# One transformer block on one Trainium2 core: eight products on zeros ahead of the first loads, K/V products of two tiles split by weight chunk, w_phi loaded from another queue, and a new unit order

## The chip, the cores and the metric

The kernel is one program on one NeuronCore of a Trainium2 chip. Five engines work side by side, each through its own queue of instructions: PE (TensorE, matrix products), DVE (VectorE), ACT (ScalarE), POOL (GpSimd) and SP (SyncE, which here only issues DMA transfers). They wait for one another on semaphores. The metric is the device time of one execution in microseconds; lower is better. Four runs of the kernel before the change gave 288.08, 289.53, 287.90 and 289.26 us, so the median is 288.67 us.

## The reference: what is computed

The input x has 2048 rows (tokens) of 640 values in bf16. Two halves follow one another, each with a layer norm without learned scale and a residual sum.

```
x1  = x + attention(layernorm(x))        # linear attention, 32 heads of 20
out = x1 + glu(layernorm(x1))            # (g * u) @ w_down, no activation

q, k, v = layernorm(x) @ wqkv            # 640 -> 3 * 640
pk      = k_head @ w_phi[head]           # 20 x 20 per head; the same for q
phi     = [softmax(pk), softmax(-pk)]    # 40 features per head
kv      = sum over tokens of phi_k^T v   # 40 x 20 per head, z = sum of phi_k
o       = (phi_q @ kv) / (phi_q @ z + 1e-6), then @ wo
```

The sum over tokens stands between the two parts of the attention: no token's output can be computed before all 2048 tokens have gone through K and V.

## The kernel before, in words

**Tiles.** The 2048 tokens are 16 tiles of 128 rows. The 640 columns of the model are 5 chunks of 128 for contraction; an output of 640 columns is two halves of 320, each in its own PSUM bank (there are 8 banks). The feed-forward part works in five blocks of tokens: 256, 512, 512, 512, 256.

**Units.** `build_graph` describes the work as named units (`G.op`), each with an engine, an emit function, an occupancy, and its reads and writes. The names matter for what follows; a number is a tile unless said otherwise.

- `wk0`, `wk2`, `wk4` load the K columns of wqkv (chunks 0-1, 2-3, 4; 160 KB per chunk), `wv0`, `wv3` the V columns, `x0`, `x1`, `x2`, ... the tokens, all on SP's queue (L259). `phr` and `ph5` load w_phi (L280), from ACT's queue.
- `WT0`..`WT4` (L345) transpose a chunk of the K weights on PE in six pieces; `WTe0`.. copies the result out of PSUM (L228). `F1_0`..`F1_4` (L366) multiply a chunk by the block-diagonal w_phi matrix `Phi`, which POOL builds (`phi0`, `phi5`, L320 and L326); `Fe1_0`.. copies it into the weight tile `Wp`. So the feature map is folded into the K weights once. `F0_0`.. does the same for the Q weights.
- `L1s`, `L1a` (L382, L385, DVE), `L1l`, `L1e` (ACT) and `xn` (L410, DVE) are the layer norm of a tile. Tiles 0 to 2 are transposed on PE (`xt`, L418, copied out by `xte`), the others by a DMA transpose on SP's queue (L426), which writes `xnT`.
- `V` and `K` (L437) are the products of a tile with the V weights and the folded K weights, ten products of 320 columns each. `Ve` copies V out, `Kx` (L455, ACT) takes the two exponentials, `Ks` (L458) and `Kr` (L461, both DVE) sum and invert per head, `Kn` (L463, POOL) scales, and `KV` (L472, PE) adds the tile's contribution to the sum over tokens, which stays in three PSUM banks from tile 0 to tile 15.
- `Q` (L493), `N` (L526), `o`, `O` (L569) and `h` are the second half of the attention; `U` (L608), `g`, `u`, `D` (L626), `y` (L638) and `w` (L640) the feed-forward part. Tile 15's `D` and `y` are made in two halves of 320 columns, so that the last output is small.

**What sets the order.** The order on each engine is not written by hand. `schedule` is a list scheduler: it steps through time, and each engine that is free takes the ready unit with the lowest key; `take` gives it PSUM banks. The keys come from the string `TUNED`, which holds `name:key` or `name:key:1`; the `:1` picks the second engine where a unit has a choice (ACT or DVE for a copy out of PSUM). `schedule` also keeps a counter `bw` for the transfers: the bytes of all DMAs pass one after another at a fixed rate. `emit` then works out the semaphore waits, and each engine runs its list strictly in order. A different table therefore changes every queue, also where no line of code has changed.

**The start before the change.** SP issues x1, x0, x6, wk0, wk2, wv0, x2, wk4, wv3, x4. PE begins with WT1 and WT0, which need wk0. DVE takes the tiles' norms in the order 1, 0, 6, 7, 2, 3, ...

**The loads inside the K/V part.** SP's queue also carries the transposes of tiles 3 to 15 and, between them, the remaining tokens, six transposes of the Q weights (`wqt`), and the weights of the output projection and of gate and up (`wo`, `wg`, `wu`, 320 to 480 KB each), paced by `PACE` so that a load follows a certain transpose.

## Time and profile before

| | before |
|---|---|
| median of four runs | 288.67 us (287.90 to 289.53) |
| the profiled execution's own time | 288.08 us |
| its span | 286.4 us |
| PE busy | 273.3 us, 95% of the span |
| DVE busy | 179.6 us, 63% |
| ACT busy | 105.6 us, 37% |
| POOL busy | 61.4 us, 21% |
| first product on PE | 7.29 us |
| last product's result taken up by DVE | 283.72 us |

The profiled execution took 1.7 us more than its span, which covers what lies around the first and the last instruction. The page gives busy times per engine, the span in 40 slices, and groups of instructions by source line. The chain of waits goes back from the last instruction to whatever released each step. The timeline lists instructions by start and duration, with the idle time before them and what ended it. PE's busy time counts instructions in flight, so neighbours overlap: a single 320-column product is shown with 299 ns, but ten of them in a row take 1.36 us in the chain.

### The profile page before, as it was taken

To read this page: it belongs to the slowest core of one execution; us is meant where nothing else is said; L and a number is where in the kernel's file an instruction comes from. 1 tells how busy PE (TensorE), PEld (TensorE's weight loads), DVE (VectorE), ACT (ScalarE), POOL (GpSimd) and SP (SyncE) were. 2 spreads that over 40 slices of the span, in tenths; PEclk is the share of its full clock that TensorE was granted. 3 is DMA by queue.
4 is the path that set the end of the run, shared out by engine and by line. 5 is a ranking of instruction groups with operands and counts; after the bars stand their busy time and mean duration, and the time that the engine had idled before them with its cause. 6 is when DMAs were issued, how large, how long until landed. Compare 5 with 4: busy or idle time off the path is not lost.

```text
span 286.4 us, 4973 instructions
## 1 busy us (share of the span) xinstructions
PE 273.3 (95%) x2047; PEld 182.2 (64%) x2063; DVE 179.6 (63%) x365; ACT 105.6 (37%) x186; POOL 61.4 (21%) x67
## 2 busy tenths in 40 slices
PE   0999999889999999999999999999999999999996
PEld 0976778668555678855565576544677545667774
DVE  3799799976367978993769825315736725233432
ACT  2877656353777761523204103033101222421010
POOL 7005479689013223000210010000002010000000
PEclk9999999999999999999999999999999999999999
DMA  7548178990002376512133211200022120100101
GB/s 208 208 99 201 51 133 184 269 353 7 0 0 48 62 211 166 79 35 48 25 70 48 46 46 49 69 0 2 1 69 71 46 48 0 24 2 3 66 14 57
DMA packets 44766, 22.31 MB, mean 78 GB/s; under 512 B 35783, under 2 KB 43463, under 8 KB 44743
## 3 DMA queue, kind: packets, MB, share of 16 engines
q1 hardware_dynamic: 43984, 21.96, 31.4%
q8 instruction: 16, 0.26, 0.4%
q10 hardware_dynamic: 759, 0.03, 0.2%
q14 instruction: 7, 0.06, 0.1%
HBM read 11.01 MB, written 2.62 MB: 48 GB/s over the span
## 4 chain that ended last, share of the span: by engine, by line
PE 88%; DMA 5%; DVE 4%; ACT 1%; issue 1%; SPq 0%; DVEq 0%
PE ps L608 36%; PE ps L626 18%; PE ps L437 10%; PE ps L569 8%; PE ps L493 7%; PE ps L526 4%; PE ps L472 3%; DMA xnT<-xn 3%; DMA scratch<-in_A_wqkv_dram 2%; DVE SR L458 2%; PE ps L366 1%; PE ps L345 1%; DVE xn L410 1%; ACT ev L455 0%; SPq L259 0%
## 5 line engine op out<-in xcount | busy, mean ns | idle before, releaser
L608 PE MATMUL ps<-xnT,Wgu 128*128 128x512 bf16 (+1 forms) x588 | 106.2, 335 | 0.6
L608 PEld LDWEIGHTS ps<-xnT,Wgu 128*128 128x128 bf16 x600 | 58.3, 98 | 42.4 <-DVE ev L616 0.8
L613 ACT ACTIVATE scratch<-ps 128x512 bf16<-128x512 f32 (+1 forms) x60 | 30.6, 511 | 95.9 <-PE ps L608 83.8
L616 DVE TENSOR_TENSOR ev<-ps,scratch 128x512 bf16<-128x512 f32 (+1 forms) x60 | 33.4, 575 | 34.7 <-PE ps L608 18.6
L626 PE MATMUL ps<-Wp,ev 128*128 128x320 bf16 x384 | 53.5, 299 | 0.0
L437 PE MATMUL ps<-Wp,xnT 128*128 128x320 bf16 x320 | 46.3, 299 | 2.2 <-DMA xnT<-xn 2.0
L626 PEld LDWEIGHTS ps<-Wp,ev 128*128 128x128 bf16 x384 | 37.5, 98 | 14.7
L463 POOL TENSOR_TENSOR ev<-ev,SR 128x1280 bf16<-128x1280 bf16 x16 | 37.4, 2365 | 27.1 <-DVE SR L461 27.1
L437 PEld LDWEIGHTS ps<-Wp,xnT 128*128 128x128 bf16 x320 | 30.3, 98 | 14.8 <-DMA xnT<-xn 3.6
L638 DVE SCALAR_TENSOR_TENSOR Wp<-ps,rs,x_all 128x640 bf16<-128x640 f32 (+1 forms) x17 | 14.4, 845 | 32.0 <-PE ps L626 32.0
L558 POOL TENSOR_TENSOR scratch<-scratch,sm 128x640 bf16<-128x640 f32 x12 | 15.2, 1270 | 59.3 <-DVE sm L555 41.0
L588 ACT ACTIVATE xn<-x_all,mv 128x640 bf16<-128x640 bf16 x16 | 13.2, 825 | 34.8 <-DVE mv L582 34.8
L458 DVE TENSOR_REDUCE SR<-ev 128x64 f32<-128x1280 bf16 x16 | 23.5, 1469 | 3.7 <-ACT ev L455 3.4
L502 ACT ACTIVATE eqT<-ps 128x512 bf16<-128x512 f32 x40 | 21.6, 594 | 11.2 <-PE ps L493 11.1
L455 ACT ACTIVATE ev<-ps 128x640 bf16<-128x640 f32 x32 | 20.7, 705 | 12.2 <-PE ps L437 11.4
L569 PE MATMUL ps<-Wo,scratch 128*128 128x320 bf16 x160 | 24.0, 299 | 0.0
L583 POOL TENSOR_SCALAR ln<-mv 128x1 f32<-128x1 f32 x16 | 3.3, 208 | 93.8 <-DVE mv L582 92.1
L493 PE MATMUL ps<-xnT,Wp 128*128 128x512 bf16 x96 | 22.8, 379 | 0.2
L569 PEld LDWEIGHTS ps<-Wo,scratch 128*128 128x128 bf16 x160 | 15.5, 98 | 7.0 <-DMA scratch<-scratch 0.3
L526 PEld LDWEIGHTS ps<-KVm,eqT 128*128 128x128 bf16 x192 | 12.9, 98 | 4.4 <-issue 0.2
L573 DVE TENSOR_TENSOR x_all<-ps,x_all 128x640 bf16<-128x640 f32 x16 | 13.1, 820 | 4.1 <-PE ps L569 4.0
L526 PE MATMUL ps<-KVm,eqT 128*128 128x154 bf16 (+1 forms) x192 | 15.5, 221 | 0.1
(51 smaller groups left out, 193.0 us busy)
## 6 DMA issues: line engine op xcount, KB each, us to landing
out_dram<-Wp SPq DMA_DIRECT2D x15, 160.0 KB, 1.8
x_all<-in_A_x_dram SPq DMA_DIRECT2D x7, 320.0 KB, 3.6
Wgu<-in_B_w_gate_dram SPq DMA_DIRECT2D x5, 384.0 KB, 5.7
Wgu<-in_B_w_up_dram SPq DMA_DIRECT2D x5, 384.0 KB, 5.7
Wp<-in_B_w_down_dram SPq DMA_DIRECT2D x4, 480.0 KB, 5.5
scratch<-in_A_wqkv_dram SPq DMA_DIRECT2D x2, 320.0 KB, 5.3
Wp<-in_A_wqkv_dram SPq DMA_DIRECT2D x1, 480.0 KB, 6.6
Wo<-in_A_wo_dram SPq DMA_DIRECT2D x1, 480.0 KB, 4.8
```

Source lines behind the costliest of these rows:

```text
L437: ins = e.matmul(pb(b, hb)[:, 0:320], lhsT=T["xnT"][:, c, P * t:P * (t + 1)], rhs=T["Wp"][:, kind, c, 320 * hb:320 * (hb + 1)], start=(c = ...
L455: G.op("act", "Kx%d_%d" % (t, s), lambda e, s=s, b=b, ek=ek: e.activation(out=T["ek"][:, ek.slots[0], s, :].rearrange("p (b n) -> p b n", ...
L458: G.op("dve", "Ks%d" % t, lambda e, ek=ek, sr=sr: e.tensor_reduce(out=T["SR"][:, sr.slots[0], 0, :], in_=T["ek"][:, ek.slots[0], :, :].rea ...
L463: G.op("pool", "Kn%d" % t, lambda e, ek=ek, sr=sr: e.tensor_tensor(out=T["ek"][:, ek.slots[0], :, :].rearrange("p s (h f) -> p (s h) f", f ...
L493: ins = e.matmul(pb(b)[:, 0:n], lhsT=T["Wp"][:, 0, i, P * c:P * (c + 1)], rhs=T["xnT"][:, i, o0:o0 + n], start=(i == 0), stop=(i == NC - 1))
L502: G.op("act", "Qx%d_%d_%d" % (q, c, s), lambda e, s=s, c=c, o0=o0, n=n, b=b: e.activation(out=T["eqT"][:, s, c, o0:o0 + n], in_=pb(b)[:, 0 ...
L526: ins = e.matmul(pb(b, y)[:, 22 * h0:22 * (h0 + j1 - j0)], lhsT=T["eqT"][:, s, c, P * t:P * (t + 1)], rhs=T["KVm"][:, OFF[s, c] + j0:OFF[s ...
L569: ins = e.matmul(pb(b, hb)[:, 0:320], lhsT=T["oT"][:, oT.slots[0], c, :], rhs=T["Wo"][:, c, 320 * hb:320 * (hb + 1)], start=(c == 0), stop ...
L608: ins = e.matmul(pb(b)[:, 0:n], lhsT=T["Wgu"][:, gu, c, P * ft:P * (ft + 1)], rhs=T["xnT"][:, c, o0:o0 + n], start=(c == 0), stop=(c == NC ...
L613: G.op("act", "g%d_%d" % (bi, ft), lambda e, pg=pg, gt=gt, n=n: e.activation(out=T["gt"][:, gt.slots[0], 0:n], in_=pb(pg)[:, 0:n], func=AF ...
L616: o_ = G.op("dve", "u%d_%d" % (bi, ft), lambda e, pu=pu, gt=gt, hh=hh, ft=ft, n=n: e.tensor_tensor(out=T["hh"][:, hh.slots[0], ft, 0:n], i ...
L626: ins = e.matmul(pb(b, hb)[:, 0:320], lhsT=T["hh"][:, hh.slots[0], ft, P * tt:P * (tt + 1)], rhs=T["Wd"][:, ft, c0 + 320 * hb:c0 + 320 * ( ...
```

## The change

Five things change in the code; the table `TUNED` is replaced as a whole.

1. Before anything else DVE clears a tile `zero` (128x512), and PE makes eight products of 512 columns from it into a PSUM bank that nobody reads (`warm`).
2. The V and K products of tiles 0 and 1 become five units each, one per weight chunk (`V0_0` to `V0_4`, and so on). Each waits for its own chunk of the weights alone. The V weights come in three transfers (2, 2 and 1 chunks) in place of two.
3. `phr` and `ph5` go to SP's queue. `ph5` loads 40 rows in place of 128, into a tile that POOL clears first (`ph50`).
4. Tile 15's last product is cut 320, 192, 128 columns in place of 320, 320.
5. In `schedule` the counter `bw` starts at 2.2 and goes at 240 up to 5.0 and at 370 from there, in place of 340 throughout. The new keys in `TUNED` come from a search with noise.

```diff
+TSPLIT = (0, 1)
+NWARM = 8
+LASTCUT = [(0, 320), (320, 512), (512, 640)]
...
-    for n_, (a, b_) in enumerate(((0, 3), (3, 5))):
+    for n_, (a, b_) in enumerate(((0, 2), (2, 4), (4, 5))):
         dma("sp", "wv%d" % a, lambda a=a, b_=b_: T["Wp"][:, 2, a:b_, :],
...
-    dma("act", "phr", lambda: T["phr"][0:120, :, :],
+    dma("sp", "phr", lambda: T["phr"][0:120, :, :],
...
-    dma("act", "ph5", lambda: T["ph5"][:, :], lambda: T["A_wphi"].rearrange("h d f -> (h d) f")[512:640, :], 5, [ph5_b], key=-99)
+    G.op("pool", "ph50", lambda e: e.memset(T["ph5"][:, :], 0.0), 0.2, LP, [], [ph5_b], -99.2)
+    dma("sp", "ph5", lambda: T["ph5"][88:128, :], lambda: T["A_wphi"].rearrange("h d f -> (h d) f")[600:640, :], 2, [ph5_b],
+        reads=[ph5_b], key=-98.4)
...
+    G.op("dve", "zero", lambda e: e.memset(T["zero"][:, :], 0.0), 0.2, LD, [], [z_b], -200)
+    def warm(e):
+        for _ in range(NWARM):
+            ins = e.matmul(pb(wm_b)[:, 0:512], lhsT=T["zero"][:, 0:P], rhs=T["zero"][:, :], start=True, stop=True)
+        return ins
...
     def proj(kind, t, name, key):
         b = Buf(name, "psum", 2)
+        parts = [(c, c + 1) for c in range(NC)] if t in TSPLIT else [(0, NC)]
+        for c0, c1 in parts:
...
-        G.op("pe", name, f, mm_c(*[320] * 10), LT, [xT_b[t]] + wp_b[kind], [b], key)
+            G.op("pe", name if len(parts) == 1 else "%s_%d" % (name, c0), f, mm_c(*[320] * (2 * (c1 - c0))), LT,
+                 [xT_b[t]] + wp_b[kind][c0:c1], [b], key)
...
-            halves = [(0, 320), (320, 640)] if t == last else [(0, 640)]
+            halves = LASTCUT if t == last else [(0, 640)]
...
-                bw = max(bw, now + 1.5) + o.dma / 340.0
+                bw = max(bw, now + 1.5)
+                bw += o.dma / (240.0 if bw < 5.0 else 370.0)
```

The new orders, as far as they are spoken of below:

- SP: x0, wv4, phr, wk4, x1, ph5, wk2, wk0, wv0, x2, wv2, x4, x6, then the transposes and paced loads; among them xt12, xt13, wg2, wu1, xt14, wu2, wg1, wu3, wg3, xt15.
- PE: warm, WT4, xt0, WT3, F1_4, WT2, WT1, WT0, F1_3, xt1, V0_0, F1_0, V0_1, F1_1, V0_2, F1_2, V0_3, K0_0, V0_4, K1_0, K0_1, K1_1, K0_2, V1_0, K0_3, V1_1, K0_4, V1_2, xt2, V1_3, K1_2, V1_4, K1_3, K2, V2, K3, V3, K1_4, V5, ...; later ... K15, V14, KV12, F0_2, KV13, V15, Q0_4, Q0_1, KV14, Q0_3, KV15, Q0_2, Q0_0, ...
- DVE from Ks0 to Kr10: Ks0, xn5, xn6, xn4, xn7, L1s8, Kr0, ..., Ks5, xn8, Kr5, Ks3, xn11, Kr3, ..., xn9, ..., xn10, ..., Kr7, xn12, xn13, Ks9, Kr8, xn14, Ks10, xn15, Kr10.
- POOL's scalings: Kn0, 2, 1, 5, 3, 4, 6, 7, 8, 10, 9, 11, 12, 13, 14, 15.
- Copies out of PSUM: of the V tiles DVE has tile 15 alone (before: 0, 1, 11, 15); of the Q folds it has none (before: three); of the K folds it has three (before: one).

## The prediction

> **What bounds the kernel now.** I read the busy rows and the 40 slices first, to see which engine fills the span.
>
> ```profile
> span 286.4 us, 4973 instructions
> PE 273.3 (95%) x2047; PEld 182.2 (64%) x2063; DVE 179.6 (63%) x365; ACT 105.6 (37%) x186; POOL 61.4 (21%) x67
> PE   0999999889999999999999999999999999999996
> ```
>
> PE is busy from the second slice to the last, so time can be won only where PE is empty, slow or waiting. The chain of waits shows where.
>
> ```profile
> 2.17 5.06 DMA scratch<-in_A_wqkv_dram
> 7.24 0.05 issue
> 7.29 1.46 PE ps L345 x12
> ...
> 12.14 0.34 PE ps L345 x6
> 12.48 0.29 PE ps L366 x7
> ...
> 18.81 0.60 ACT ev L455
> 19.41 0.02 issue
> 19.44 1.49 DVE SR L458
> ...
> 29.11 0.68 PE ps L472 x12
> 29.80 1.36 PE ps L437 x10
> ...
> 54.99 4.92 DMA xnT<-xn
> 59.90 0.05 issue
> 59.95 1.53 PE ps L437 x10
> ```
>
> PE starts at 7.29, when wk0 lands. Twelve transposes take 1.46 there (0.122 each), six take 0.34 (0.057) at 12.14: PE runs at half rate at first. At 54.99 the chain leaves PE: a tile's transpose ends a wait.
>
> The chain also gives a price for every unit: K or V tile 1.36 (two of its ten products 0.27), KV 0.68, fold 0.29, six weight transposes 0.34, a tile's five transposes 0.28, Q or a 512-token U 1.08, a 256-token U 0.545, N 0.36, O 1.36, D 3.26. I call a unit's start minus the sum of all units before it its **delay**. PE's timeline has K1 at 17.50, after 8.07 of work (5 x 0.34, 3 x 0.28, 5 x 0.29, 3 x 1.36): delay 9.4. Q0_0 starts at 73.51 after 60.9 (32 K and V 43.5, 16 KV 10.9, ten folds 2.9, transposes 2.5, one Q 1.1): delay 12.6. At the end, 283.65, all work is 270.8: delay 12.8. So 9.4 us go at the start, 3.2 in the K/V part, 0.2 in the 210 us after it.
>
> The DVE timeline of the K/V part shows what makes tiles late there.
>
> ```profile
> 48.17 1.10 DVE L410 TENSOR_SCALAR xn<-x_all,mv,rs 128x640 bf16<-128x640 bf16 x1
> 49.19 1.48 DVE L458 TENSOR_REDUCE SR<-ev 128x64 f32<-128x1280 bf16 x1
> 50.58 1.08 DVE L410 TENSOR_SCALAR xn<-x_all,mv,rs 128x640 bf16<-128x640 bf16 x1
> 51.59 1.47 DVE L458 TENSOR_REDUCE SR<-ev 128x64 f32<-128x1280 bf16 x1
> 52.98 0.43 DVE L410 TENSOR_SCALAR xn<-x_all,mv,rs 128x640 bf16<-128x640 bf16 x1
> ```
>
> POOL's timeline shows what ran beside them.
>
> ```profile
> 37.47 14.01 POOL L463 TENSOR_TENSOR ev<-ev,SR 128x1280 bf16<-128x1280 bf16 x6 [5.56 <-DVE SR L461]
> ```
>
> Two normalisations took 1.10 and 1.08 while POOL scaled (until 51.48); the one at 52.98, with POOL idle, took 0.43.
>
> **The start.** Warm products: a clear and eight products of 512 columns; at half rate (0.427 each, four times a cold 128-column one) 3.4 us, all before the first weights. They end near 4.7 and cover nothing else. The half rate cost PE about 2 us: its first 29 transposes and 21 fold products took 4.57 (7.29 to 11.86) against 2.5 at the later prices. What remains of that gain is set by who is late next: the loads.
>
> The loads run one after another. wk0 landed at 7.23 with 960 KB ahead of or in it; wv3, issued at 5.00 with 6.9 to landing, at 11.9, 1600 KB later: 343 KB per us. In the new order wk0 has 1306 KB, 346 more, so it lands at 8.2. The favourable end is issue alone: seven SP issues at about 0.48 from 0.79 put wk0's at 4.15; with a free 160 KB load's 2.3 to landing and 0.45 more for its size, 6.9. I take 8.2, the loaded row; x1, wk4 and wk2 come earlier, so by then PE has done WT4, xt0, WT3, F1_4, WT2.
>
> From wk0 on ACT is late next: two transposes 0.7, copies WTe0, WTe1, xte1, Fe1_0, Fe1_1, Fe1_2 at 0.6 to 0.7 each 3.9, waits 0.4. So K0_2 can start 5.0 after wk0, at 13.2, with 6.1 of work ahead of it: delay 7.1. V0_2 (wv2, 640 KB later, 10.1, with 4.0 ahead) and xt2 (x6, 1600 KB later, 12.9, then 0.8 of statistics and 0.4 of normalising; 7.8 ahead) are covered. K2 also needs xte2, which stands behind Kx0_0 on ACT: 0.3 more. I put the delay at K2 at **7.4** against 9.4, a gain of 2.0 (3.4 with the favourable landing). Moving phr behind wv4 on SP costs its issue, 0.65 by ACT's timeline, inside the 0.48-spaced issues; phi0 waits for it (2.6 to landing from 1.7: 4.3) and stands behind POOL's masks, ready near 6.2, before F1_4. ph5 follows x1 and lands near 5.7; phi5 is now behind phi0. The extra clears (0.2 each) stand before the first x tile on DVE and inside POOL's start.
>
> **The K/V part.** DVE hands over all V copies but one and three Q folds and takes two more K folds: 3 + 3 - 2 = 4 copies of 0.75, 3.0 off DVE and onto ACT, which had over 6 us free of 15 between 30 and 45. But POOL's scalings now collide with more normalisations. Ks0 follows Kx0_0, xte2 and Kx0_1 as before (19.44, 2.0 after K0's end at 17.40); K0_4 has 7.5 ahead, so it ends at 15.0 and Ks0 starts at 17.0. From there to Kr10 DVE has 11 sums at 1.40, 10 reciprocals at 0.46, 12 normalisations at 0.36, 8 tiles' statistics at 0.79 + 0.12 (spacings in the timeline): 31.6. Eight of the normalisations (tiles 8 to 15) now stand where POOL has scalings queued; at the 0.66 that the two rows above lost, 5.3. Bounds: nothing, and 15.3, if each loses a whole scaling (2.35 less its own 0.44). Kr10 then ends at 53.9. POOL does 10, 9, 11, 12, 13 one after another, 5 x 2.33, so KV13 cannot start before 65.7, with 56.4 ahead of it on PE: delay **9.3** against 12.6.
>
> The Trainium skill, "SBUF — State Buffer", section "Who interferes with whom", says that DVE's fast modes and GpSimd share a port pair as an exclusive lock: the later one stands still until the other is done. The rows agree (1.10 from 48.17 ends 0.2 after a scaling's end). By it a normalisation met at random would lose half a scaling, 1.18, eight 9.4, and KV13 would stand at 69.8, delay 13.4, the K/V gain gone and more: a rule that speaks against this change.
>
> Transposes behind weights: xt14 follows wg2 and wu1, xt15 wu2, wg1, wu3, wg3. Before, the transposed tile of the chain landed 4.92 after issue behind three such loads. xn15 ends by 53.2; behind 1536 KB at 343 it lands by 60, and K15 has 52.7 ahead: it asks for a delay of 7.3 only. Hidden.
>
> **After the K/V part** the units are the same and the loss was 0.2; KV15 leaves three Qs before the first N, 3.2 us, where DVE needs 2.1 for the three KVe. I leave 0.2.
>
> **The tail.** The last y took 0.55 for 320 columns, a 640 one 0.89: 128 columns cost 0.35, a gain of 0.2. Cutting 320 in 192 and 128 costs PE 12 x 2.5 ns = 0.03. Nothing hides this; it stands at the end.
>
> Sum: delay 12.8 to 9.5, 3.3, and 0.2 at the tail: 3.5. On the profiled execution 288.08 - 3.5 = 284.6; that one is 0.6 below the median of 288.67, so **285.2** in the terms of the median.
>
> **Rivals.**
> - *No wait in the K/V part*: normalisations fall into POOL's gaps. For it: four of the earlier ones did (34 to 36.8). Delay 7.4 + 0.2 and the favourable landing up to 1.4 less: 12.8 - 7.6 + 0.2 = 5.4, 283.3, down to 281.9.
> - *The zeros do not lift the rate.* PE is nearly empty between 4.7 and 8; if it is at half rate again from wk0 on, up to 2 us of the old loss come back, through Kx0 and Ks0 to all that follows: 287.2. The trace shows one rise only, about 4 us after PE's first work. The Trainium skill, "TensorE: Matmul & The Clock Gate", Part 1, has it that a busy window of about 3.4 us, not counted from the first product, lifts the clock, and an idle one drops it; the rise in the trace agrees, no run here shows the drop. By it the eight products are just one window long, and the sum could be either 285.2 or 287.2.
> - *Slower: DVE stands behind POOL.* Place: normalisations 8 to 15; price: what each loses, times eight, straight to KV13. At 1.2 each the result is before's time; at 1.5 (12 us) Kr10 ends at 60.6, KV13 stands at 72.4, delay 16.0, and the time is 288.67 + 3.4 - 0.2 = 291.9. It decides from 1.35 each. For it: six scalings ran back to back from 37.47. Against: DVE that is held up feeds POOL later, which opens gaps; two of sixteen lost 0.66.
>
> **How the numbers follow.** Half a per cent, 1.4 us, is about what a measurement of this kernel tells from no change: below 287.2 faster, above 290.1 slower. Chances: forecast 0.52 (its own range 284.0 to 286.6); no wait 0.16; half rate 0.12, mostly on the faster side; DVE behind POOL 0.20, of which 0.04 end faster, 0.09 same, 0.07 slower. Faster 0.52 + 0.16 + 0.09 + 0.04 = 0.81, same 0.03 + 0.09 = 0.12, slower 0.07. The range takes in the first two, the half rate and part of the last: 282.4 to 288.4.
>
> **What the profile after would show.** Right: transposes at 0.06 each from the first, WT1 near 8.2, K2 near 16.6, KV13 near 66 ended by POOL's L463, the first N near 76, a last y of 0.35. Wrong: WT1 near 7 or below, 0.107 a transpose after the zeros, normalisations of over 1.5, a wait of PE after 80 us, or PE waiting for a transposed tile for over 1 us.

## The result, and the profile after

The changed kernel takes 289.42 us in the median (286.92 to 291.14, 45 runs), the kernel before 288.97 (286.66 to 291.04, 71 runs, those beside the experiments included). The ratio is 1.0018, with a 95% interval of 1.0003 to 1.0033: if anything slower by 0.2%, where 1.2% of gain was forecast. The forecast was 285.2, so 4.2 us of gain are missing. The profiled execution took 288.29 us against 288.08.

The first lines of the page of the kernel after: span, busy time, and PE's share in 40 slices.

```profile
span 286.6 us, 5018 instructions
PE 276.2 (96%) x2067; PEld 182.1 (64%) x2083; DVE 183.8 (64%) x364; ACT 108.7 (38%) x191; POOL 58.8 (21%) x66
...
PE   6899998999999999999999999997999999999996
```

PE now starts in the first slice (the products on zeros), but there is a new dent in the 28th slice, near 195 us, where PE never waited before.

The chain of waits of the kernel after (start, duration, what it was).

```profile
3.59 4.70 DMA scratch<-in_A_wqkv_dram
...
30.92 2.48 DVE xn L426
...
40.23 3.62 DMA xnT<-xn
43.85 0.05 issue
43.90 1.53 PE ps L455 x10
...
56.24 11.62 POOL ev L484 x5
...
194.17 5.10 DMA scratch<-scratch
199.31 1.53 PE ps L590 x10
```

Four places hold the end up: the load wk2 (landing at 8.29), a normalisation of 2.48 and a transposed tile near 31 to 44, the five scalings of POOL in a row to 67.86, and a transpose of the attention's second half (oT13) that took 5.10.

PE's waits in the same execution (in all, times, longest), those on transposed tiles, on POOL and on oT13:

```profile
PE ps L590 <- DMA scratch<-scratch: 1.7, 1, 1.7
PE ps L455 <- DMA xnT<-xn: 1.4, 2, 0.8
...
PE ps L493 <- POOL ev L484: 0.5, 2, 0.3
```

PE's timeline of the kernel after shows the start (start, duration, count; in brackets the idle time before and what ended it).

```profile
5.09 0.82 PE L361 MATMUL ps<-ident,scratch 128*128 128x128 bf16 x6 [0.26 <-DMA scratch<-in_A_wqkv_dram]
...
8.33 0.51 PE L361 MATMUL ps<-ident,scratch 128*128 128x128 bf16 x6 [1.89 <-DMA scratch<-in_A_wqkv_dram]
...
8.98 1.17 PE L361 MATMUL ps<-ident,scratch 128*128 128x128 bf16 x18
```

WT4 ran at half rate; then PE waited 1.9 for wk2. In this execution the transposes after the wait ran at full rate, eighteen in a little over 1 us.

Where the two profiled executions differ is seen from the delay. Below it is counted product by product, at 0.0558 us for 128 columns, 0.1358 for 320 and 0.2158 for 512, the prices behind the chain's 0.34, 1.36 and 1.08. On this scale the three values that the prediction read for the kernel before (9.4, 12.6, 12.8) are 9.49, 13.05 and 13.66.

| delay at | before | after | forecast change | measured change |
|---|---|---|---|---|
| K2 | 9.49 | 8.30 | -2.0 | -1.2 |
| Q0_0, behind the K/V part | 13.05 | 11.94 | -3.3 | -1.1 |
| O13, near 200 us | 13.61 | 14.13 | -3.3 | +0.5 |
| D14_0, near 279 us | 13.66 | 14.19 | -3.3 | +0.5 |

The tail gives back a little: from the last output's start on DVE to the end of the span it was 2.7 us and is 2.3. So of the 3.8 that are missing at D14_0, 0.8 are lost at the start, 1.4 in the K/V part (it lost 3.6 in both kernels, where 1.9 was forecast) and 1.6 behind it, where the single unit O13, 120 us later, lost 1.8.

### The profile page after: what moved, and what is told of

Its sections match the earlier page's. It is cut to its first block, busy times and chain, and to the rows that moved or that the text cites. A ratio compares the mean times of both kernels' runs of the same rounds, so it can differ in the third digit from the quotient of the medians.

```text
span 286.6 us, 5018 instructions
## 1 busy us (share of the span) xinstructions
PE 276.2 (96%) x2067; PEld 182.1 (64%) x2083; DVE 183.8 (64%) x364; ACT 108.7 (38%) x191; POOL 58.8 (21%) x66
## 4 chain that ended last, share of the span: by engine, by line
PE 81%; DVE 6%; POOL 5%; DMA 5%; ACT 1%; issue 1%; SPq 0%; DVEq 0%; POOLq 0%
PE ps L629 35%; PE ps L648 18%; PE ps L514 7%; PE ps L455 7%; PE ps L590 7%; POOL ev L484 4%; PE ps L547 4%; DVE xn L426 3%; DVE SR L479 2%; DMA scratch<-scratch 2%; DMA scratch<-in_A_wqkv_dram 2%; DMA xnT<-xn 1%; PE ps L493 1%; DVE SR L482 1%; PE ps L382 1%
## 5 line engine op out<-in xcount | busy, mean ns | idle before, releaser
L648 PE MATMUL ps<-Wp,ev 128*128 128x320 bf16 (+2 forms) x396 | 54.0, 295 | 0.0
L484 POOL TENSOR_TENSOR ev<-ev,SR 128x1280 bf16<-128x1280 bf16 x16 | 37.5, 2367 | 28.3 <-DVE mv L401 17.0
L579 POOL TENSOR_TENSOR scratch<-scratch,sm 128x640 bf16<-128x640 f32 x10 | 12.7, 1271 | 123.7 <-DVE sm L576 110.2
L660 DVE SCALAR_TENSOR_TENSOR Wp<-ps,rs,x_all 128x640 bf16<-128x640 f32 (+3 forms) x18 | 14.6, 810 | 26.2 <-PE ps L648 26.1
L560 DVE RECIPROCAL sm<-ps 128x32 f32<-128x32 f32 x16 | 5.6, 352 | 16.0 <-PE ps L547 15.9
L514 PEld LDWEIGHTS ps<-xnT,Wp 128*128 128x128 bf16 x100 | 9.5, 98 | 9.4
L547 PEld LDWEIGHTS ps<-KVm,eqT 128*128 128x128 bf16 x192 | 12.8, 98 | 4.1
```

The source lines that it names most:

```text
L484: G.op("pool", "Kn%d" % t, lambda e, ek=ek, sr=sr: e.tensor_tensor(out=T["ek"][:, ek.slots[0], :, :].rearrange("p s (h f) -> p (s h) f", f ...
L514: ins = e.matmul(pb(b)[:, 0:n], lhsT=T["Wp"][:, 0, i, P * c:P * (c + 1)], rhs=T["xnT"][:, i, o0:o0 + n], start=(i == 0), stop=(i == NC - 1))
L547: ins = e.matmul(pb(b, y)[:, 22 * h0:22 * (h0 + j1 - j0)], lhsT=T["eqT"][:, s, c, P * t:P * (t + 1)], rhs=T["KVm"][:, OFF[s, c] + j0:OFF[s ...
L648: ins = e.matmul(pb(b, hb)[:, 0:w], lhsT=T["hh"][:, hh.slots[0], ft, P * tt:P * (tt + 1)], rhs=T["Wd"][:, ft, c0 + w * hb:c0 + w * (hb + 1 ...
```

## The experiments

### What the zeros do

**Zeros alone.** The kernel before with the clear and the eight products on zeros in front, all else in its order.

```diff
+    G.op("dve", "zero", lambda e: e.memset(T["zero"][:, :], 0.0), 0.2, LD, [], [z_b], -200)
+    G.op("pe", "warm", warm, 0.43 * NWARM, LT, [z_b], [wm_b], -200)
```

> The kernel before with the clear and the eight products on zeros alone; every other unit keeps its place. Theory A (the prediction's): the zeros lift PE's rate before wk0 lands, so the 29 transposes and 21 fold products that took 4.57 us (7.29 to 11.86) take about 2.5 to 3; K1 starts near 15.9 instead of 17.5 unless ACT's copies hold it, and the time falls by 1 to 2 us. Theory B (PE is covered by ACT's copies and by DVE in the K/V part): the first transposes take 0.06 each, but K0 or the K/V part gives the time back, and the time moves by less than 0.5 us. Theory C (the rate does not rise): transposes at 0.12 each as before, no change.

Over its twelve executions the median is 291.85 (286.88 to 296.19), against 289.51 for the kernel before beside them; over the four shortest alone the ratio is 0.9986 (0.9947 to 1.0025). So the zeros alone show no gain. The profiled execution is among the long ones, so the trace is used for its first 13 us alone. PE's timeline there:

```profile
1.24 3.59 PE L347 MATMUL ps<-zero 128*128 128x512 bf16 x8 [1.24 <-DVE zero L342]
6.89 1.46 PE L357 MATMUL ps<-ident,scratch 128*128 128x128 bf16 x12 [2.06 <-DMA scratch<-in_A_wqkv_dram]
```

Twelve transposes still take 1.46, as without zeros. PE stood idle for 2.06 between the zeros and the data. Whether the rate had risen in between, no product shows; when the data came it was half. K1's delay was 9.53 (9.49 before).

**The change without the zeros.**

```diff
-    G.op("pe", "warm", warm, 0.43 * NWARM, LT, [z_b], [wm_b], -200)
```

> The changed kernel without the eight products on zeros; the order of all else is the same. In the changed kernel WT3 started at 8.34 when wk2 landed, at 0.06 a transpose. Theory A: without the zeros PE is at half rate until some 4 us after WT4 (5.1), so until 9 to 12: K2 starts 0.5 to 2 us later than 17.40, and the time rises by as much. Theory B: the load of wk2 and wk0 and ACT's copies set K0_2 whatever the rate; K2 moves by less than 0.5 us and the time stays.

289.84 (288.43 to 292.84), ratio 1.0006 (0.9984 to 1.0029). The delay at K2 is 10.63. So on the changed kernel the zeros can't be told from nothing by the time, although one trace has 2.3 less delay with them. The reason is in the next two runs, which have the changed kernel's start and something else changed later.

**O13 later, and a strided normalisation.** In the first, the order of PE and DVE is held, and only O13 moves behind U2_11_1 and U2_10_1. In the second, the normalisation of tiles 8 to 15 reads and writes every second element, then the others.

```diff
+    # PE, around 195 us: U2_5_1 U2_11_1 U2_10_1 O13 U2_9_1 ... in place of U2_5_1 O13 U2_11_1 U2_10_1 U2_9_1 ...
```

> The changed kernel with O13 two units (2.16 us) later on PE; g2_11 and u2_7 trade places with hc13 and h13. In the changed kernel PE waited 1.7 us before O13 for the transpose of tile 13, which took 5.1 us to land; beside it one instruction packet of 16 KB held a DMA engine for 1.68 us. Theory A: this wait is in every execution, because the packet comes at the same place of the program; with O13 behind two more units it is gone, and the time falls by 1.2 to 1.7 us. Theory B: it was one execution's accident, or the next wait takes its place: less than 0.5 us.

```diff
-            return e.tensor_scalar(out=T["xn"][:, xb.slots[0], :], in0=T["x"][:, t, :],
+            v = (lambda a: a.rearrange("p (n two) -> p two n", two=2)) if t >= 8 else (lambda a: a)
+            return e.tensor_scalar(out=v(T["xn"][:, xb.slots[0], :]), in0=v(T["x"][:, t, :]),
```

> The changed kernel with the normalisations of tiles 8 to 15 reading and writing every second column, first the even, then the odd ones; same values. In the changed kernel four of these eight took 2.48, 1.35, 2.48 and 1.08 us beside POOL's scalings, against 0.44 alone. Theory A (DVE's fast form stands still while POOL scales): in the slow form each takes about 0.75 and none over 1; DVE gains some 3 us before Kr10, KV13 comes 1.5 to 3 us earlier than 67.9, the time falls by as much, less what PE then lacks. Theory B (the long ones are due to something else): they stay long, Kr10 comes later by up to 2 us, and the time rises.

O13 later: 289.04, ratio 0.9985 (0.9959 to 1.0011). Strided: 290.56, ratio 1.0031 (1.0009 to 1.0054). What each shows of its own subject follows below; here it is their start. The busy time by stretches gives PE's granted clock (the column after POOL's). The kernel after:

```profile
8.00:11.00 3.00, 2.67 (x45) 2.35 (x45) 2.12 (x4) 1.49 (x3) 0.00 (x0) 1.00 1.05 364
11.00:14.00 3.00, 3.00 (x36) 1.86 (x36) 3.00 (x10) 3.00 (x7) 0.00 (x0) 1.00 0.41 142
```

The strided kernel in the same stretches:

```profile
8.00:11.00 3.00, 2.76 (x31) 2.77 (x32) 1.65 (x3) 0.81 (x1) 0.00 (x0) 0.59 0.96 330
11.00:14.00 3.00, 3.00 (x44) 2.49 (x42) 2.15 (x5) 2.69 (x5) 0.00 (x0) 0.84 0.42 152
```

0.41 of 3 us and 0.16 of 3 us of the strided kernel's clock are missing: 1.7 us, a stretch of 3.4 us at half rate, right after PE's wait for wk2. Its K2 has a delay of 9.40, that of the run with O13 later 9.37 (its clock is 0.74 and 0.69 in these stretches). That is before's 9.49. Among the 46 listed executions of the changed kernel, 27 have a mean clock of 0.994, which is such a stretch (0.6% of 287 us is 1.7; the mean does not say where it lies), and they take 289.65 in the mean; the 17 with a clock of 1.000 take 288.54. The profiled execution of the changed kernel is one of the lucky ones. The mean is blind to one case, a half rate that lasts from the first product on: three of the executions below have a mean of 1.000 and transposes of 0.107. Seven executions with the changed kernel's loads and eight zeros were profiled in all, two of them with other first units; their delays at K2 are 8.30, 9.08, 9.34, 9.37, 9.40, 10.27 and 10.60, 9.5 in the mean. Only the first kept its rate: in three the clock fell after the wait (9.34, 9.37, 9.40), in three the rate had not risen when wk2 came. Over these seven executions, then, the start gained nothing. A wait of some 2 us went either way: PE's idle time before wk2 was 1.89 in the one that kept its rate, and 1.74, 2.00 and 2.17 in the three that lost it.

The Trainium skill, "TensorE: Matmul & The Clock Gate", Part 1, has the activity window run free of the kernel's start, so that one kernel meets it in different phases. That one order kept its rate, lost it or never had it in these executions agrees; no run here shows the window itself.

**Sixteen zeros,** so that PE is busy until the data come: on the changed kernel and on the kernel before, the orders unchanged.

```diff
-NWARM = 8
+NWARM = 16
```

> The changed kernel with 16 instead of 8 products on zeros, all else in the same order. Theory A, the clock falls back while PE waits: the eight products end at 4.83 and PE then has 1 us of work until wk2 lands at 8.3; in the profiled executions of the strided and the O13 experiments the transposes after that took 0.107 each and K2 stood 1.1 later than in the profiled execution of the changed kernel. Sixteen products keep PE busy until 6.6 to 8.3, so the rate stays up: transposes at 0.056 in the profile, delay at K2 at most 8.4, mean granted clock 1.000 in all timed runs, and a median 0.6 to 1.1 us below that of the changed kernel (ratio to before about 0.999). Theory B, the loads alone set the start: no change, ratio 1.002; or, if the eight more products hold WT4 and xt0 up, up to 1 us more (1.005).

> The kernel before with a clear and 16 products on zeros in front and nothing else changed. With eight of them PE stood idle from 4.9 to 6.9, the first 29 transposes and 21 fold products still ran at half rate and K1 had a delay of 9.53 against 9.49 without. Theory A: sixteen products end near 7 to 8, the rate is up when wk0's transposes start, so they take 0.057, K1's delay falls by 1 to 2 to between 7.5 and 8.5 and the time by as much of it as the K/V part leaves, between 0 (all eaten by later waits there, DVE and POOL being no earlier) and 2.0: 287 to 289. Theory B: K1's delay stays near 9.5 and the ratio is 1.000.

On the changed kernel: 288.34 (287.31 to 290.84), ratio 0.9985 (0.9955 to 1.0015). K2's delay is 8.82: held up by the products themselves, but at full rate. On the kernel before PE's timeline reads:

```profile
1.24 5.56 PE L347 MATMUL ps<-zero 128*128 128x512 bf16 x16 [1.24 <-DVE zero L342]
7.01 0.84 PE L357 MATMUL ps<-ident,scratch 128*128 128x128 bf16 x12 [0.21 <-DMA scratch<-in_A_wqkv_dram]
```

Twelve transposes take 0.84 in place of 1.46, and K1's delay falls from 9.49 to 8.63. So theory A holds for the rate: it is up, and stays up, if PE is kept busy until the data come. Yet this kernel is slower than before, 291.09, ratio 1.0072 (1.0039 to 1.0105): with DVE and POOL in the same order, the K/V part lost 5.2 (8.63 at K1, 13.82 at Q0_0) where it had lost 3.6. Here an earlier start was no gain by itself.

Theory A's mean clock of 1.000 in all runs did not come: four of the twelve executions of the changed kernel with sixteen zeros have 0.994. A wait in the middle can drop the clock as well. In the profiled run of the changed kernel with sixteen zeros PE waited 2.0 us for tile 14's transpose, until 61.2; the stretches by time (clock again after POOL's column):

```profile
60.00:63.00 3.00, 1.80 (x8) 1.04 (x9) 2.73 (x3) 0.00 (x0) 3.00 (x2) 0.71 0.94 338
63.00:67.00 4.00, 4.00 (x41) 3.04 (x40) 2.41 (x4) 2.23 (x4) 4.00 (x3) 0.79 1.07 385
```

Again 1.7 us are missing. A wait of 2 cost near 4, and the K/V part of this execution lost 7.1 (8.82 at K2, 15.96 at Q0_0).

### What the loads do

**The small loads out of the way:** w_phi's two loads on ACT's queue, as before, and wv4 behind wv2. wk2 becomes SP's fourth issue in place of the seventh. The planner then also orders some units differently.

```diff
-... wv4:1.18 ... phr:1.66 ph50:1 ph5:3.1 ...
+... wv4:5.6 ... phr:0.1 ph50:1 ph5:0.2 ...
-    dma("sp", "phr", lambda: T["phr"][0:120, :, :],
+    dma("act", "phr", lambda: T["phr"][0:120, :, :],
-    dma("sp", "ph5", lambda: T["ph5"][88:128, :], ...
+    dma("act", "ph5", lambda: T["ph5"][88:128, :], ...
```

> The changed kernel with wphi's two loads back on ACT's queue at its start and wv4 behind wv2 on SP, so that wk2 is SP's fourth load and not its seventh. Theory: the small loads first make the start wait for issues: wk2 landed at 8.29 as the seventh issue. Here it is issued 1.4 us earlier, so it lands near 7.0 and wk0 near 8; WT3 starts near 7.1, K2's delay falls from 8.3 (9.4 where the rate drops) by 0.9 to 1.3; the median falls by 0 to 1.2, less where the K/V part's own limit (POOL's scalings before KV13) eats it. Rival: bytes set the landings, wk2 stays near 8.3 and nothing moves.

**284.07 us** (283.86 to 285.52), ratio 0.9841 (0.9803 to 0.9879): faster than both kernels, by more than expected. PE's timeline:

```profile
4.30 0.50 PE L361 MATMUL ps<-ident,scratch 128*128 128x128 bf16 x6
6.53 0.51 PE L361 MATMUL ps<-ident,scratch 128*128 128x128 bf16 x6 [1.73 <-DMA scratch<-in_A_wqkv_dram]
...
7.46 1.17 PE L361 MATMUL ps<-ident,scratch 128*128 128x128 bf16 x18
```

wk2 lands at 6.48 (8.29 before the move), K2's delay is 7.02. O13 does not wait.

**Only the loads moved,** the order of the four engines held to the changed kernel's:

```diff
+    # loads as above; PE, DVE, ACT and POOL chained in the changed kernel's order
```

> As the run with the small loads late (284.07, 0.984 of before), but with the order of PE, DVE, ACT and POOL held to that of the changed kernel: only the loads' places differ from it. Theory, the places of the loads did it: wk2 lands near 6.5, WT3 starts there, the delay at K2 is near 7.0 to 7.3 (8.3 in the changed kernel) and the time 284 to 285.5. Rival, the new order did it (the two last tiles' normalisations and Kr9 earlier, K1_4 earlier): K2 gains its 1.3, but the K/V part loses 3.4 again instead of 2.3 and the time is 286.5 to 288.

288.45 (286.66 to 290.88), ratio 0.9984 (0.9946 to 1.0022). wk2 lands at 6.51 and K2's delay is 6.99, as in the run above. But the K/V part loses 3.7 (10.71 at Q0_0) and O13 loses 1.4 again. The rival had the mechanism, though it expected a lower time: the loads alone are worth 1.0 us of some 5.

**w_phi's loads alone moved,** wv4 still second on SP:

```diff
-    dma("sp", "phr", ...)  dma("sp", "ph5", ...)
+    dma("act", "phr", ...)  dma("act", "ph5", ...)
```

> The changed kernel with wphi's two loads back on ACT's queue and all else where it is: wv4 stays SP's second load, so wk2 is the fifth issue instead of the seventh, after 960 KB in all. Theory, wk2 follows its issue by 4.3 to 4.7: issue at 2.65, landing near 7.2, between the changed kernel's 8.2 and the 6.5 of the runs with both moved; K2's delay at full rate 7.5 to 7.7, the time 288.6 to 289.2. Rival, bytes: wk2's landing stays at 8.1 to 8.2.

288.52 (285.93 to 290.56), ratio 0.9984 (0.9951 to 1.0016). wk2 was issued at 2.65 and landed at 7.58: between the other two, as by issue. K2's delay was 8.06, at full rate, held by ACT after wk2. The K/V part of this execution lost 5.3 (13.38 at Q0_0), with one wait of 1.8 for a transposed tile near 60 us; the clock stayed at 1.000.

**The other way round:** the kernel before with w_phi's loads on SP, ahead of all weights.

```diff
-phr:0.7 ph5:1.18            # on ACT's queue
+phr:1.3 ph5:1.4             # on SP's, behind x1 and x0; all engines chained in before's order
```

> The kernel before with wphi's two loads moved from ACT's queue to SP, behind x1 and x0 and ahead of x6, wk0 and all others; the order of the engines is that of before. Theory, the start waits for issues: two issues of 0.48 in front, so wk0 lands 0.8 to 1.0 later than its 7.24, PE starts at 8.1, the delay at K1 goes from 9.5 to 10.3 or more and the time from 288.97 to 289.5 to 290. Rival, bytes set the landings: two loads of 29 KB cost 0.1, wk0 at 7.3, no change.

The mechanism failed: wk0 was issued at 3.18 in place of 2.17 and still landed at 6.86, no later than before's 7.24. wk4 came 0.9 later (12.10), K1's delay was 9.96. The kernel nevertheless is slower than expected, 293.77, ratio 1.0174 (1.013 to 1.0219), nearly all of it in the K/V part, where the delay of the profiled execution went from 9.96 to 17.70; PE waited there four times for a transposed tile:

```profile
PE ps L437 <- DMA xnT<-xn: 3.7, 4, 2.3
```

Behind the longest wait, which ended at 62.97, the clock was 0.64 from 63 to 67. So the landing follows the issue where small loads stand in front (the changed kernel), and not where 960 KB do (the kernel before). Whether it is the issues, the bytes or the 640 packets of 40 bytes that slow a load is not settled.

**Without the zeros, with the loads moved:**

```diff
-    G.op("pe", "warm", warm, 0.43 * NWARM, LT, [z_b], [wm_b], -200)      # in the kernel of 284.07
```

> As the run with the small loads late (284.07), without the products on zeros, in the same order. Theory: the zeros are worth about 2 us of rate at the start where the wait after them is short: without them the first transposes take 0.107 to 0.12, the delay at K2 goes from 7.0 to 8.5 to 9.2 and the time to 285.5 to 286.3. Rival, as on the changed kernel (289.84 without zeros against 289.42 with): the zeros are worth nothing, 284 to 284.5.

286.97 (286.32 to 288.18), ratio 0.993 (0.9902 to 0.9959). Here the zeros are worth 2.6 (by the ratios) to 2.9 us (by the medians): K2's delay is 8.75 in place of 7.02, and O13 lost 0.8 in the profiled execution. In all six executions of 284.07 the mean clock is 1.000: there the rate outlasts the wait for wk2 (1.73 in the trace), and the zeros are worth something.

### What the order does

**Half of the scaling.** POOL scales only the first 640 of the 1280 columns of each K tile; the other half of the feature map stays unscaled.

```diff
-            out=T["ek"][:, ek.slots[0], :, :].rearrange("p s (h f) -> p (s h) f", f=DH),
+            out=T["ek"][:, ek.slots[0], 0, :].rearrange("p (h f) -> p h f", f=DH),
...
```

> The changed kernel with POOL's scaling of each K tile cut to the first 640 of its 1280 columns, so half of the scaling of the feature maps is left out; the order of all instructions is the same. Theory: POOL's scalings set the K/V part twice, by holding DVE's normalisations (xn8 2.48, xn13 2.48, xn11 1.35, xn15 1.08) and by five in a row before KV13. With 1.2 instead of 2.33 each, no normalisation takes over 1.4, KV13 starts without a wait, and the delay at Q0_0 (11.7) falls by 2.0 to 3.4 to between 8.3 and 9.7; the time falls by as much, to 286 to 287. Rival: the tiles' transposes (K9 waited 1.0 for one, V8 0.8) set it: then waits of that size stay, and the delay at Q0_0 falls by less than 1.0.

286.54 (285.49 to 288.18), ratio 0.9921 (0.9891 to 0.995), with an unlucky start (9.34 at K2). From there to Q0_0 it lost 1.2, where the changed kernel lost 3.6. The normalisations as a group:

```profile
L426 DVE TENSOR_SCALAR xn<-x_all,mv,rs x16: 349/441/624, 4.9 to 52.5; 128x640 bf16<-128x640 bf16 x16
```

The longest is 0.62, at the start; of tiles 8 to 15 none takes over 0.45, against 2.48. In this order POOL's scalings limit the K/V part, directly and through DVE. DVE's timeline of the kernel after shows the holds, DVE's waits for ACT, and the last output:

```profile
24.96 1.49 DVE L479 TENSOR_REDUCE SR<-ev 128x64 f32<-128x1280 bf16 x1 [0.60 <-ACT ev L476]
...
30.92 2.48 DVE L426 TENSOR_SCALAR xn<-x_all,mv,rs 128x640 bf16<-128x640 bf16 x1 [0.56 <-ACT rs L409]
...
48.35 2.84 DVE L426 TENSOR_SCALAR xn<-x_all,mv,rs 128x640 bf16<-128x640 bf16 x2 [0.34 <-ACT rs L409]
...
54.62 1.08 DVE L426 TENSOR_SCALAR xn<-x_all,mv,rs 128x640 bf16<-128x640 bf16 x1
...
284.28 0.35 DVE L660 SCALAR_TENSOR_TENSOR Wp<-ps,rs,x_all 128x128 bf16<-128x128 f32 x1 [0.25 <-PE ps L648]
```

POOL's timeline of the same execution:

```profile
28.55 4.67 POOL L484 TENSOR_TENSOR ev<-ev,SR 128x1280 bf16<-128x1280 bf16 x2 [4.07 <-DVE SR L482]
...
56.24 16.24 POOL L484 TENSOR_TENSOR ev<-ev,SR 128x1280 bf16<-128x1280 bf16 x7 [0.72 <-DVE SR L482]
```

The second of the two scalings from 28.55 stands from 30.87 to 33.22 in the trace. xn8 began at 30.92, 0.06 later, and ended at 33.40: it lost a whole scaling. Each held normalisation ends 0.18 to 0.19 after the scaling beside it: tiles 8, 11, 13 and 15 at 33.40, 36.48, 51.19 and 55.70, the scalings at 33.22, 36.30, 51.00 and 55.52. So each lost what was left of that scaling.

**The strided normalisation** (run above) was held as long. Its first one on DVE's timeline, with POOL's scalings from 29.65 to 34.32:

```profile
32.02 2.68 DVE L427 TENSOR_SCALAR xn<-x_all,mv,rs 128x640 bf16<-128x640 bf16 x1 [0.55 <-ACT rs L409]
...
55.05 0.54 DVE L427 TENSOR_SCALAR xn<-x_all,mv,rs 128x640 bf16<-128x640 bf16 x1
```

It costs 0.54 in place of 0.34 when POOL is idle as it begins, and gains nothing. The Trainium skill, "VectorE: DVE Perf Modes", section "Mode 2×_2P", asks for operands in SBUF and an even outermost dimension, which two interleaved halves have; the run agrees in so far as this form was held as well, 2.68 and 2.67 at the longest.

**One scaling on DVE:** K tile 11's, in the kernel of 284.07.

```diff
-        G.op("pool", "Kn%d" % t, lambda ...
+        G.op("dve" if t in (11,) else "pool", "Kn%d" % t, lambda ...
```

> As the run with the small loads late (284.07), with the scaling of K tile 11 on DVE instead of POOL. Theory, POOL's five scalings in a row before KV13 are the limit of the K/V part: four are left, so KV13 starts up to 2.3 earlier, and the delay at Q0_0 falls from 9.3 to 7.5 to 8.3; the time 282.5 to 283.5. Rival: DVE's scaling waits for POOL's, or takes as long (over 2 us), and the later sums and normalisations come as much later: no gain, 284 to 285.

286.03 (284.21 to 287.83), ratio 0.9894 (0.9862 to 0.9926): worse than 0.9841. DVE's timeline:

```profile
60.99 2.15 DVE L485 TENSOR_TENSOR ev<-ev,SR 128x1280 bf16<-128x1280 bf16 x1
```

POOL's timeline of this execution:

```profile
57.12 4.67 POOL L485 TENSOR_TENSOR ev<-ev,SR 128x1280 bf16<-128x1280 bf16 x2 [2.12 <-DVE SR L483]
63.68 2.36 POOL L485 TENSOR_TENSOR ev<-ev,SR 128x1280 bf16<-128x1280 bf16 x1 [1.89 <-DVE SR L483]
66.87 4.67 POOL L485 TENSOR_TENSOR ev<-ev,SR 128x1280 bf16<-128x1280 bf16 x2 [0.83 <-DVE SR L483]
```

POOL was busy until 61.79; DVE's scaling took 2.15 and pushed the next sums back, so POOL stood idle twice and Kn13 began at 66.87. That is the rival's mechanism, read from the longest of ten executions, whose start was poor too (8.70 at K2 against 7.02) and in which xn8 was held for 2.63; how the loss of 2.0 in the median divides is not shown. The Trainium skill, "SBUF — State Buffer", section "Who interferes with whom", counts a DVE operation with two inputs in SBUF among those that contend with POOL's reads; the 2.15, with POOL busy for its first 0.80, fits that, but no run has this scaling with POOL idle to compare.

**The order alone:** the changed kernel's loads, with the engines in the order of the kernel of 284.07.

```diff
+    # loads as in the changed kernel; PE, DVE, ACT and POOL chained in the order of the kernel of 284.07
```

> The changed kernel with its loads where it has them (wv4 and wphi's two ahead of wk2 on SP's queue), and PE, DVE, ACT and POOL in the order of the run with the small loads late (284.07). Theory, loads and order each have their share: the loads alone gave 0.998 of before, 1.0 us less than the changed kernel; so the order alone gives the rest, about 3: xn15 ahead of Ks10 on DVE lets POOL's row of five start earlier, the K/V part loses 2.3 instead of 3.4, and the time is 285.5 to 286.5. Rival, the two need each other (an order that only pays when wk2 lands early): 288 to 289.5.

287.09 (285.51 to 289.29), ratio 0.9922 (0.989 to 0.9953). K2's delay was 9.08, Q0_0's 11.34, so the K/V part lost 2.3, and O13 did not wait. The order alone is worth 2.3 in the median and the loads alone 1.0, both together 5.3: the sum of the parts is 2 short. One difference on record is the clock, 1.000 in all six executions with both and in four of eleven with the order alone; why the two help one another is not shown.

**The end of DVE's row alone,** and then **everything but that end.**

```diff
-  DVE: xn14 Ks10 xn15 Kr10 Kr9 Ks11      POOL: Kn8 Kn10 Kn9 Kn11
+  DVE: xn14 xn15 Ks10 Kr9 Kr10 Ks11      POOL: Kn8 Kn9 Kn10 Kn11
```

> The changed kernel with one swap: DVE does xn15, Ks10, Kr9, Kr10 in place of Ks10, xn15, Kr10, Kr9, and POOL does Kn9 ahead of Kn10. Nothing else moves. Theory: this swap is most of the order's gain. xn15, issued while POOL is busy with one scaling, shares xn14's wait instead of meeting a later one (1.08 before), Kr9 comes 0.5 earlier, so POOL's row of five starts 1.0 to 1.6 earlier, KV13 too, and the tile 15's transpose lands earlier: Q0_0 1.0 to 1.6 earlier, the time 287.8 to 288.4. Rival: the swap is worth nothing (289.4), the order's gain came from the first units (K1_4, xt2, F1_0).

```diff
-  PE: ... V1_2 xt2 V1_3 K1_2 V1_4 K1_3 K2 V2 K3 V3 K1_4 ...
+  PE: ... V1_2 K1_2 V1_3 xt2 V1_4 K1_3 K1_4 K2 ...; V0_1 ahead of F1_0, WT3 ahead of xt0; ACT to match
   DVE and POOL at their end as in the changed kernel
```

> The complement of the swap of xn15: the changed kernel with its own loads and its own end of DVE's and POOL's row (Ks10, xn15, Kr10, Kr9; Kn10 ahead of Kn9), and all other units in the order of the run with the small loads late (K1_4 three units earlier, xt2 two later, V0_1 ahead of F1_0, WT3 ahead of xt0, and ACT's evacuations to match). Theory: the order's gain (287.09 against 289.42) came from these units: they shift DVE's row against POOL's, so that xn8 no longer starts as a scaling starts (2.48 in every execution with the old order, 0.45 with the new one), and the waits of 0.8 for tile 8's and 1.0 for tile 9's transpose go. Then the time is 287 to 288 and xn8 takes 0.45. Rival: only both together, 289 or more.

The swap: 290.58 (288.64 to 292.07), ratio 1.0042 (1.0013 to 1.0072), no gain. In its profiled execution, which also had a start of 10.27, two of the last four normalisations were held (DVE's timeline; each line is a held one and a free one):

```profile
50.66 2.75 DVE L426 TENSOR_SCALAR xn<-x_all,mv,rs 128x640 bf16<-128x640 bf16 x2 [0.67 <-ACT rs L409]
...
55.18 2.74 DVE L426 TENSOR_SCALAR xn<-x_all,mv,rs 128x640 bf16<-128x640 bf16 x2
```

The rest of the order: 286.19 (285.59 to 287.66), ratio 0.9906 (0.9868 to 0.9943). DVE's timeline where xn8 stands:

```profile
32.20 0.71 DVE L426 TENSOR_SCALAR xn<-x_all,mv,rs 128x640 bf16<-128x640 bf16 x1
```

xn8 takes 0.71 in place of 2.48 and PE no longer waits for tiles 8 and 9. Although this execution had a poor start (10.60 at K2), it lost 1.1 to Q0_0, not 3.6; from Ks0 to Q0_0 it took 56.1 us, against 57.8 in the changed kernel. So the order of the first units, moved by a few places near 15 us (K1_4 and xt2 on PE, and ACT's copies with them), decides how DVE's row meets POOL's near 31 us; which of these moves does it was not tried singly. In the eight full-scaling executions with the changed kernel's first units xn8 took 2.48 every time (2.68 in the strided form); in the six with the new first units 0.45, 0.45, 0.45, 0.60, 0.71, and once, with tile 11's scaling on DVE and a start of 8.70, 2.63. In the five others it began 0.2 to 0.5 before the end of the running scaling and ended 0.2 behind it; in this one it began 0.13 before the end and lost the whole of the next.

**What is left.** The kernel of 284.07 with KV11, KV12 and KV13 each a unit later on PE, and the store w5_0 issued behind oT13's transpose.

```diff
-  PE: KV10 F0_0 KV11 K15 V14 KV12 F0_2 KV13 V15 Q0_4      SP: oT11 w5_0 oT13
+  PE: KV10 F0_0 K15 V14 KV11 F0_2 KV12 V15 KV13 Q0_4      SP: oT11 oT13 w5_0
```

> As the run with the small loads late (284.07) with two more moves: PE does KV11, KV12 and KV13 each one unit later (K15 and V14 ahead of KV11, V15 ahead of KV13), and SP issues the store w5_0 behind the transpose oT13 instead of 0.4 ahead of it. Expected: the wait of 1.2 for POOL before KV11 goes, since there is other work for PE until Kn11 ends at 60.6 and Kn13 at 65.2; Q0_0 1.3 earlier. oT13 lands in 2.6 instead of 3.1 to 5.1, so O13 never waits: nothing in the execution profiled before, 0.5 to 1 in others. The time 282.5 to 283.2. Rival: the units put ahead wait themselves (K15 for its transposed tile, V14 for a free accumulator): 284.

**283.18 us** (282.78 to 284.51), ratio 0.9805 (0.9769 to 0.9841), the lowest time; its interval meets that of 284.07 (0.9803 to 0.9879), so the step between the two is not certain. PE's waits in it:

```profile
PE ps L361 <- DMA scratch<-in_A_wqkv_dram: 0.6, 1, 0.6
PE ps L455 <- DMA xnT<-xn: 0.3, 1, 0.3
...
PE ps L493 <- POOL ev L484: 0.2, 1, 0.2
```

The wait of 1.2 for POOL is 0.2 now. The second move did not do what it was for: oT13 took 3.5 with no store ahead of it, and O13 just escaped a wait.

### O13's transpose

In the run with O13 later its wait went, and another came six units behind it, for the transposed tile that follows from O13, now late itself; PE's timeline:

```profile
209.01 3.18 PE L629 MATMUL ps<-xnT,Wgu 128*128 128x512 bf16 x14 [0.97 <-DMA xnT<-xn]
```

The wait moved, it did not go. What makes oT13 slow is in the DMA view, by queue and by transfer, of the kernel after from 193 to 200:

```profile
q8 instruction: 1, 0.02, 1.5%
q14 instruction: 1, 0.01, 0.3%
...
scratch<-scratch SPq DMA_TRANSPOSE x1, 5.1
```

The same view of the kernel before, 207 to 212, has no packet on an instruction queue:

```profile
q1 hardware_dynamic: 914, 0.45, 33.5%
...
scratch<-scratch SPq DMA_TRANSPOSE x1, 2.6
```

1.5% of 16 engines over 7 us is 1.7 us of one engine, about what O13 waits. With one such packet each, of 1.0 us on q8 in the run with the loads alone moved and of 0.3 us on q14 in the kernel of 284.07, the transpose took 4.7 and 3.3.

All 19 traces say the same. Of their transposes issued after 130 us, when the loads are over, 214 had no instruction packet within 2.6 us of their issue, and none of these took over 2.71; 112 had one, and 72 of them took over 3.0, up to 5.13. In the fifteen traces of the changed kernel and its variants oT13 took 4.1 to 5.1 in the nine that had a packet of about 1.0 us or more there, and O13 lost 0.8 to 1.9 in eight of these (in the ninth it stood later); it took 3.0 to 3.5 in the six whose packet was of 0.3 to 0.5, and O13 lost nothing. So the two go together. That the packet is the cause is not shown: no run moved these packets.

## Why the prediction was wrong, point by point

**The start: the failed step is "I take 8.2, the loaded row; x1, wk4 and wk2 come earlier".** wk2 landed at 8.29 and wk0 at 9.16. With small loads in front the queue didn't run at the 343 KB per us of the loaded row: 986 KB were down at 8.29, where before 960 were at 7.24. Behind wk2 the rate held (320 KB in 0.87), so the landing of wk2 is the term that was mis-sized, by 1.0. The favourable end, 6.9 by issue alone, was no nearer. With the loads moved K2's delay was 7.0, close to the 7.4 forecast, and in the profiled execution of the changed kernel K2 stood 8.2 behind wk0's landing, where the prediction has 8.4: the terms after the landing (ACT's copies, folds) were sound.

**"The zeros do not lift the rate" was given 0.12 and is what most executions do.** PE had 0.6 to 1.2 us of work between the zeros' end at 4.83 and wk2, and of the seven profiled starts three lost the rate again, by the drop that the rival named, and three never had it. The late landing and the lost rate together made a gain of 2.0 into none in the mean. Both hang on what the first big load has in front of it.

**The K/V part: the failed step is the sum 31.6 + 5.3 from Ks0 to Kr10, as if DVE waited for nothing but POOL there.** Mechanism and price were right: the prediction charged eight normalisations 0.66 each, 5.3; in the profiled execution tiles 8, 10, 11, 13 and 15 lost 2.0, 0.1, 0.9, 2.0 and 0.6 beyond 0.44, the other three nothing: 5.8. But the loss sits on few: two lost 2.0 each. The whole stretch from Ks0 to Kr10's end took 38.3 in place of 36.9, since DVE stood idle for 1.5 in it, each time for ACT (0.60, 0.56 and 0.34 in the lines above), which the prediction put at nothing. It also began 0.9 late (17.89), so Kr10 ended at 56.17, not 53.9, and KV13 stood at 67.91, not 65.7, ended by POOL's L484 as forecast. xn8 and xn9 were late for PE too, which lost 0.8 at tile 8 and 1.0 at tile 9, and the chain goes through the second of these (43.90) and ACT back to DVE's row at 48.35: a path that the prediction didn't follow. So the part lost 3.6, as before, where 1.9 was forecast: 1.8 at these two tiles, 1.1 at POOL's scalings and the rest in small pieces. xt15, which it did follow, took 6.8 to land and was hidden, as it said.

**The exclusive lock of the Trainium skill** ("SBUF — State Buffer", section "Who interferes with whom"), weighed there at 1.18 each and 9.4 in sum, has the mechanism: each held normalisation ended just behind a scaling. But a mean over random meetings is not what an order written down meets: with the old first units and plain normalisations xn8 took 2.48 and xn11 1.35 in all seven traces.

**"I leave 0.2" after the K/V part failed:** 2.2 were lost there, 1.8 of them at O13. Before, it was 0.6 on the scale of the table, so the reading of 0.2 was low as well. The prediction named a wait of PE after 80 us and normalisations of over 1.5 as signs that it is wrong, and both came. Nothing in the trace before shows the wait at O13. In the changed kernel's order O13 stands about 3.4 behind oT13's issue, and oT13 took 3.5 to 5.1.

**The tail** was right: a last output of 0.35.

**The slower rival** (1.35 per normalisation from which it decides) did not come: the mean was 0.72.

**The noise.** The prediction took one execution's order of events for the kernel's. In the old order the clock, single holds (tile 12 or 13) and O13's transpose each shift by 1 to 2 us from one execution to another; the executions of each of the two lowest versions (six each) lie within 1.8 us, those of the changed kernel (45) within 4.2.

## What to carry to other kernels

Products on zeros buy a rate, not time: the rate can be lost again if PE then waits some 2 us for data, so look at what stands ahead of the first big load, and at many executions, not at one. Where two engines hold one another for whole instructions, ask which one comes first at each meeting; an order moved by a few units at 15 us was worth 3 us, while an earlier start under an unchanged order was worth 1.0 in one run and less than nothing in another. When a search hands out a table, try its parts one at a time: here code, loads and order together hid kernels that are 1.6 and 2% faster.

## What the hardware showed that was not expected

- A wait of 2.0 us in the middle of the K/V part cost 1.7 more, as 3.4 us at half rate (clock 0.71 and 0.79 in the stretches from 60 to 67).
- A normalisation that began 0.06 us after one of POOL's scalings took 2.48; begun 0.2 to 0.3 before the end of one, it took 0.45.
- A DMA transpose of 128 x 640 issued after 130 us took 2.6 to 2.7 in every case without a packet of an instruction queue beside it, and up to 5.1 with one.
- Two loads of 29 KB in all, put ahead of the weights in the kernel before, did not delay the first weights that PE needs, and still cost 1.7%, most of it in the K/V part.
